# One transposing transfer becomes three TensorE transposes and a copy, with the later steps of the plan in another order

## The chip, the cores and the metric

The kernel runs on one core of a Trainium2 chip. The metric is the time of one execution on the device in microseconds (us), taken over several runs; the median counts. One further execution was recorded by the hardware profiler, and its rows are what the views of the profile show.

## What is computed

Clustered attention followed by a two-layer SiLU network. Four batches of 8 heads, 768 positions, head size 64; a query sees a key only if both have the same nearest of 16 centroids.

```python
q_assign = np.argmax(np.einsum('bhsd,hcd->bhsc', q_n, c_n), axis=-1)
k_assign = np.argmax(np.einsum('bhsd,hcd->bhsc', k_n, c_n), axis=-1)
mask = q_assign[:, :, :, None] == k_assign[:, :, None, :]
scores = np.where(mask, scale * np.matmul(q, k.transpose(0, 1, 3, 2)), -1000000000.0)
attn = softmax(scores)
x = np.matmul(attn, v).transpose(0, 2, 1, 3).reshape(B * S, H * D)     # 3072 x 512
h = x @ w_in                                                          # 512 -> 2048
out = (h * (1.0 / (1.0 + np.exp(-h)))) @ w_out                        # 2048 -> 512
```

The inputs and the output are float32; inside, operands are float16 and sums float32 in PSUM.

## The kernel before, in words

The whole order of the work is written out by hand. `plan` (L815) is a list of some 1,600 words, and the loop at L894 turns each word into the instructions of one step, in that order. An engine takes its own instructions in the order of the list; between engines only the data and the buffers decide. So TensorE, VectorE (DVE), ScalarE (ACT), GpSimd (POOL) and the queue of SyncE (SP), which issues nearly all transfers, are five lists that run beside one another and wait where they must.

A word is a step's name, a number, and behind a dot the engine (A, D or P) or the PSUM bank. For the steps z and o the letter isn't read (L799 to L803); for hi, v, ce, pe and u it chooses the engine.

For head n (n = 0 to 31, eight to a batch):

- `r` (L92) loads q and k, two transfers; `hi` (L103, L105 or L107 by engine) and `lo` (L112, VectorE) split them into two float16 parts.
- `ht` (L121) turns them by a transposing transfer on SyncE's queue into the tile `ab`.
- `l` (L159) multiplies them by the centroids on TensorE, `ls` (L168), `mx` (L188) and `ge` (L197) on VectorE find the nearest one.
- The result goes back into `ab` as additional rows. For heads 8 to 15 by `cm` and `ce` (L226, L237, L239, L240); for heads 16 on by `cs` (GpSimd, L204), `cx` (a transposing transfer on SyncE, L213, into `cdt`) and `cv` (a transfer that GpSimd issues, L217).
- `vl` (L271) loads v, and `v` (L277, L279) casts it.

Attention goes by units of one head, one half of the queries and two blocks of keys: `qk` (L336, two matmuls of 384 columns into `pS`, two buffers) and `ex` (the exponential on ScalarE, L341). `pv` n (L353, 36 matmuls) multiplies the exponentials of a pair of heads by v; n counts batch, half of the queries and pair of heads, so that 12 to 15 are the four pairs of batch 1's second half. `nm` (L363, L365) normalises the result on VectorE into `xn`.

The normalised rows must be turned before the network can use them, into one of the four row blocks of the tile `xt`. There are two ways, and the plan names one for each pair:

```python
def xn_t(i, c, bk=None):
...
    for t in range(NM):
        nc.tensor.transpose(px[:, ts(t, 128)], xn[:, 2 * t : 2 * t + 2, :].rearrange("p h d -> p (h d)"), ident)
def xn_d(i, c):
...
    nc.sync.dma_start_transpose(
        xts[b, c][:, i % H // 2, :].rearrange("p (t n) -> p t n", t=NM), xn.rearrange("p n d -> p (n d)")
    )
```

The first is the step `pt`, three transposes on TensorE into PSUM, followed by the step `pe` (`xn_ev`, L376), the copy into `xt` by ScalarE (L383) or VectorE (L385). The second is the step `xd`, one transposing transfer on SyncE's queue (L392). The first layer of the network, for batches 0 and 1, is `e` (L401, four matmuls of 384 columns, one for each row block of `xt`, in order: the fourth reads the last pair's rows), `t` (tanh on ScalarE, L413) and `g` (the gate on VectorE, L416). Steps e48 to e63 belong to batch 1's second half. Batches 2 and 3 form the same products with seven block products for eight: sums `T` and `ws`, products `y` (L467), mixing copies and sums `u` (L479, L481, L483) and `s` (SiLU on ScalarE, L489). The second layer is `m` (L559, eight matmuls), with the sums `S` (L572) on VectorE, and `z` and `o` (L581, L587, L590), which scale the result and send it out.

Buffers that bind steps together: `xn` 3, `hl` 4, `P` 13 (exponentials), `ab` 12, `cdt` 4, `tn` 3, and eight PSUM banks, two pairs of which hold `pS`.

Of the kernel before, what the change touches and what calls it, by code (L numbers as in the profile page):

```python
# [29 lines left out]
def kernel(  # L30
# [655 lines left out]
    def step(op, n, eng, banks):  # L686
# [167 lines left out]
        t58 e59.2 g58 t62 g62 t53 g53 hi25.A qk108 ex108 lo27 cx23 vl19 S22 t59 qk104 hi26.P ex104 cx22 e51.1 t51 g51
        m21.0 qk105 z20.A m22.3 ex105 v19.P qk110 ex110 vl22 vl27 m26 qk111 ex111 xd16 o20 l24.1 vl21 qk128 ex128
        e55.3 qk109 ex109 g59 e52.2 t52 cv22 lo26 ls24 S24 g52 qk113 ex113 z21.D lo25 pv17.1 nm17 r28 ht27 hi28.D
        v21.P r30 e54.2 t54 ht26 qk130 ex130 qk112 ex112 t55 cv23 m25 mx24 g54 qk116 e63.1 g55 ex116 qk124 r31 pv18.2
        ex124 nm18 z22.A qk127 ge24 ex127 qk126 ex126 v22.P e57.3 t57 m27.2 o23 g57 xd17 t63 hi30.D vl23 qk118 ex118
        g63 ht25 qk114 ex114 m23 o21.D v23.D lo28 v27.P qk117 ex117 l26.3 ls26 r29 cs24 cx24 qk115 e50.1 ex115 qk119
        ex119 e49.0 t49 ws5 qk138 pv19.3 lo30 ex138 t50 g49 vl29 g50 qk123 ex123 qk121 ex121 e48.0 l25.1 t48 ls25 mx25  # L860
        g48 qk122 ex122 m24 qk120 ge25 cv24 nm19 cs25 vl26 ex120 l27.1 ls27 qk125 m31.0 mx27 S33 qk129 ge27 ex125
        hi29.D pv20.3 mx26 ex129 vl24 qk132 ex132 qk136 ex136 m37 qk142 z30.D ex142 ge26 ht30 cx25 e61.1 nm20 cv25
        qk133 ex133 m32.3 lo29 ws6 ht28 t61 ws8 o30 qk139 ex139 g61 S31 qk134 S32 ex134 pv21.3 qk137 xd18 S43 nm21
        l30.1 cs27 cx27 qk135 cs26 S41 ls30 m36 ex137 xd19 ex135 cx26 xd21 qk140 ex140 ht29 z31.A pv22.3 qk141 ex141
        o22 v26.D qk143 S34 ws0 nm22 m35 ex143 hi31.P qk146 ex146 pv23.1 z32.D o33 qk148 ws1 ex148 qk149 xd20 ws12 ws2
        xd22 ws13 m41.2 z40.A ex149 m33 nm23 ws14 xd23 cv27 vl25 m34 qk154 ex154 m47 mx30 ge30 o31.A S42 qk145 ex145
        qk147 l28.3 o32 ex147 lo31 ws9 y161.1 ht31 l29.0 qk155 ex155 m46 z41.A cv26 qk150 qk144 ls28 ex150 ls29 mx29
        T20 T21 ex144 m45 mx28 y167.3 z42.A o43 y177.4 ws7 u170.A y197.4 m42.0 u190.D y171 u160.A u161.A y191 u171.A
        m44 ws15 T22 T23 ge29 y172 y162 y166 ws10 u191.A s160 S44 ws3 y176 s170 u162 u172 ge28 m43 o41.D o42 y165 u163
        y192 y196 s190 v29.D u192 o40 y164 y174 y163 y175 s162 s161 l31.2 u173 y187.3 s163 u180.D y195 s172 y181.0  # L870
        ls31 u181.A vl31 s173 y194 u193 y207.1 y173 y201.2 s171 y182 y186 cs30 s192 y237.4 u200.D u201.D cx30 y202
        s180 y193 s193 y206 u182 ws11 s200 s191 cs28 y184 s182 y185 y217.4 u202 y204 u183 u230.A y205 y231 u203 s183
        y183 s202 u210.A y221.3 u231.D y227.1 s203 v24.D cs29 cx29 y211 v31.A u220.D y203 y232 u211.A u221.D y236 s230
        y216 u232 y212 s210 u212 y222 y226 s220 u222 y235 y234 s181 v25.A s201 cx28 cv28 y214 u233 s233 y215 u213 y225
        u223 s232 s213 y224 s223 s212 mx31 m51.0 z50.A y223 ge31 s222 y233 s231 pv24.2 y213 s221 s211 m61.1 S53 S51
        S52 qk156 ex156 cs31 m52.3 qk153 ex153 m56 z51.A qk151 S54 ex151 qk152 nm24 m57 S63 ex152 qk172 ex172 m55
        z52.D cv30 qk162 ex162 cv29 qk161 ex161 vl28 v28.D m67 qk158 S61 o53 m54 vl30 z60.D ex158 qk171 ex171 qk181
        pv25.2 ex181 qk157 ex157 qk160 ex160 m53 qk159 S62 ex159 S73 nm25 qk174 m66 ex174 cx31 cv31 qk165 ex165 qk164
        ex164 pv26.2 qk163 ex163 S71 o50 o51.D nm26 xd26 xd25 qk167 ex167 m62.3 o52 qk166 ex166 m71.2 qk169 ex169
        qk168 v30.P pv27.0 ex168 z61.D qk173 qk170 ex173 m65 ex170 o60 qk189 nm27 S64 xd27 ex189 qk179 pv28.3 S72  # L880
        ex179 qk177 qk175 nm28 z62.D ex177 m63 S74 o63 qk178 ex175 ex178 z70.A qk176 ex176 m72.0 xd24 o70 qk182 ex182
        m76 qk184 ex184 qk183 ex183 pv29.3 nm29 xd29 qk180 ex180 qk185 ex185 m64 o62 z71.D qk190 ex190 qk188 ex188
        pv30.0 nm30 qk186 ex186 qk187 ex187 m77 qk191 ex191 m75 pv31.3 nm31 z72.D m73 xd28 pt31.0 o73 y241.3 m74
# [44 lines left out]
```

## Time and profile before

| | |
|---|---|
| runs before | 297.19 us median of 3 (296.39 to 299.04) |
| profiled execution | 297.06 us, with a span of 295.2 us from its first to its last instruction |
| granted TensorE clock | 1.00 |
| TensorE (PE) busy | 285.8 us (97%), 3353 matmuls |
| ScalarE (ACT) busy | 245.1 us (83%) |
| VectorE (DVE) busy | 224.5 us (76%) |
| GpSimd (POOL) busy | 70.1 us (24%) |
| transposing transfers on SyncE's queue | 24 ht, 22 xd, 16 cx |

A row of the timeline has the start in us from the beginning of the span, the length, the engine, the line of the kernel, the operation, what it writes and reads, and how many instructions were merged. In brackets stands how long the engine was idle before it and for whom it waited. A row of groups has the busy time and the mean length of one in ns, then the idle time ahead of the group. Matmuls overlap: one of 384 columns is shown with 0.326 us, and the next starts 0.163 us after it. "SPq" is SyncE's queue, with the time that issuing a transfer took there; how long it took to land is told apart from that.

### The profile page before, as it was taken

The page shows a single profiled execution, that of the slowest core. Times are in us where ns is not written, and L with a number is a line of the kernel's source. Part 1 is how long each engine was busy: PE and PEld are TensorE (multiplying, and loading weights), DVE is VectorE, ACT ScalarE, POOL GpSimd, SP SyncE. Part 2 cuts the span into 40 slices and gives each one's busy share as a digit, 9 for nine tenths or more (in the row PEclk, how much of TensorE's full clock was granted, in tenths as well). Part 3 has the DMA queues.
Part 4 walks back from the last instruction along what each step waited for, and adds up shares of the span by engine and source line. Part 5 has one row for each costly group of instructions (what it writes and reads, how often), then busy time and mean ns, then how long its engine had stood idle before and what let it go on. Part 6 is the DMA issues. An engine that isn't in the chain of part 4 may idle for free.

```text
span 295.2 us, 8436 instructions
## 1 busy us (share of the span) xinstructions
PE 285.8 (97%) x3353; PEld 208.2 (71%) x3353; DVE 224.5 (76%) x489; ACT 245.1 (83%) x431; POOL 70.1 (24%) x118
## 2 busy tenths in 40 slices
...
GB/s 207 290 273 232 178 195 189 216 248 196 189 265 153 182 177 196 187 195 188 178 231 194 189 141 96 197 48 143 40 30 2 64 64 76 73 36 3 36 56 124
DMA packets 76166, 44.11 MB, mean 149 GB/s; under 512 B 54288, under 2 KB 72496, under 8 KB 76128
## 3 DMA queue, kind: packets, MB, share of 16 engines
...
HBM read 27.30 MB, written 6.29 MB: 114 GB/s over the span
## 4 chain that ended last, share of the span: by engine, by line
PE 79%; DMA 7%; ACT 5%; DVE 4%; issue 2%; SPq 1%; POOLq 0%; DVEq 0%; ACTq 0%
PE pS L336 19%; PE xb L559 18%; PE ph L401 11%; PE pO L353 10%; PE gd L467 5%; PE psN L159 3%; PE yb L559 3%; DMA ab<-cd 3%; PE gx L467 3%; PE po L498 2%; PE gy L467 2%; ACT P L341 2%; DMA raw<-in_q_dram 1%; PE wb L559 1%; DVE hl L112 1%
## 5 line engine op out<-in xcount | busy, mean ns | idle before, releaser
L341 ACT ACTIVATE P<-pS 128x768 f16<-128x768 f32 x192 | 150.0, 816 | 17.4 <-PE pS L336 15.5
L336 PE MATMUL pS<-ab 128*128 128x384 f16 x384 | 87.1, 326 | 1.3 <-DMA ab<-cd 0.6
L401 PE MATMUL ph<-xt,win_s 128*128 128x384 f16 x256 | 49.8, 326 | 1.5 <-DMA xt<-xn 1.3
L336 PEld LDWEIGHTS <-ab 128*128 128x128 f16 x384 | 33.4, 98 | 16.5 <-issue 3.0
L353 PEld LDWEIGHTS <-P 128*128 128x128 f16 x1152 | 39.8, 97 | 4.4 <-DVE cd L239 0.4
L353 PE MATMUL pO<-vt,P 128*128 128x65 f16 x1152 | 41.2, 193 | 0.0
L416 DVE SCALAR_TENSOR_TENSOR gt<-tn,ph 128x384 f16<-128x384 f32 x64 | 34.0, 549 | 9.5 <-ACT tn L413 9.0
L559 PEld LDWEIGHTS <-gt 128*128 128x128 f16 x352 | 34.3, 98 | 7.4
L401 PEld LDWEIGHTS <-win_s 128*128 128x128 f16 x256 | 24.7, 98 | 17.0 <-issue 1.2
L112 DVE SCALAR_TENSOR_TENSOR hl<-raw,hl 128x768 f16<-128x768 f32 (+3 forms) x35 | 32.1, 917 | 0.6 <-ACT hl L103 0.4
L413 ACT ACTIVATE tn<-ph 128x384 f32<-128x384 f32 x64 | 30.2, 503 | 2.3 <-PE ph L401 2.1
L105 POOL TENSOR_SCALAR hl<-raw 128x768 f16<-128x768 f32 (+1 forms) x12 | 24.5, 2044 | 29.8 <-DVE mxn L188 14.6
L559 PEld LDWEIGHTS <-s 128*128 128x128 f16 x264 | 25.6, 98 | 5.3 <-DVE s L572 0.3
L559 PE MATMUL xb<-wout_s,gt 128*128 128x256 f16 x176 | 22.6, 273 | 0.0
L159 PEld LDWEIGHTS <-ab 128*128 128x128 f16 x496 | 18.0, 97 | 4.8 <-DMA ab<-hl 0.5
L559 PE MATMUL xb<-wc,s 128*128 128x256 f16 x160 | 20.7, 273 | 0.0
L363 DVE RECIPROCAL zr<-pO 128x6 f32<-128x6 f32 x32 | 6.1, 192 | 19.1 <-PE pO L353 18.9
L581 ACT ACTIVATE ot<-xb 128x256 f32<-128x256 f32 x33 | 12.6, 386 | 8.8 <-PE xb L559 8.6
L204 POOL TENSOR_SCALAR od<-od 128x96 f16<-128x96 f16 x16 | 9.8, 610 | 40.6 <-DVE od L197 40.4
L159 PE MATMUL psN<-stk,ab 128*128 128x32 f16 (+1 forms) x496 | 19.1, 186 | 0.1
L572 DVE TENSOR_TENSOR s<-gt 128x1024 f16<-128x1024 f16 x22 | 15.7, 716 | 4.5 <-PE xb L559 2.7
L365 DVE TENSOR_TENSOR xn<-pO,zr 128x384 f16<-128x384 f32 x32 | 17.8, 558 | 1.4 <-DMA xt<-xn 0.3
(128 smaller groups left out, 413.6 us busy)
## 6 DMA issues: line engine op xcount, KB each, us to landing
...
```

Source lines behind the costliest of these rows:

```text
L105: nc.gpsimd.tensor_scalar(out=o, in0=i, scalar1=QS, scalar2=None, op0=ALU.mult)
L112: nc.vector.scalar_tensor_tensor(out=hl[:, s, 1, :], in0=raws[job.name][:, s, :], scalar=QS, in1=hl[:, s, 0, :], op0=ALU.mult, op1=ALU.sub ...
L159: nc.tensor.matmul(L[:, n % 2, :, n // 2], ab[:, i, :], stk[:, job.groups[i // 3][0], x : x + w], start=(x == 0), stop=(x + w == 2 * HC),)
L336: nc.tensor.matmul(pS[:, e, 0:HALF], abs_[kj.name][:, kn, :], rhs, start=True, stop=True)
L341: nc.scalar.activation(out=P, in_=pst.pop(u)[:, :, 0:HALF], func=AF.Exp, bias=0.0, scale=ESC)
L353: nc.tensor.matmul(o[:, (2 * t + h) * VW : (2 * t + h + 1) * VW], Ps[i + h, c, j // 2][:, j % 2, ts(t, 128)], vtb[(i + h) % 13][:, j, 0:VW ...
L365: nc.vector.tensor_tensor(out=xn, in0=ov[:, :, 0:D], in1=zr.unsqueeze(2).to_broadcast([128, 2 * NM, D]), op=ALU.mult)
L401: nc.tensor.matmul(ph[:, 0:HALF], win_s[:, r, ts(fb, 128)], xts[b, c][:, r, :], start=(r == 0), stop=(r == NR - 1))
L413: nc.scalar.activation(out=tn, in_=phs[b, c, fb][:, 0:HALF], func=AF.Tanh, bias=0.0, scale=0.5)
L416: nc.vector.scalar_tensor_tensor(out=gt[:, fb, NM * c : NM * c + NM, :].rearrange("p t n -> p (t n)"), in0=tns.pop((b, c, fb)), scalar=1.0 ...
L467: nc.tensor.matmul(o[:, 0:HALF], w[:, r, :], x[:, r, :], start=(s in (7, 1) and r == 0), stop=(r == 1), skip_group_check=True)
L559: nc.tensor.matmul(o, self.lhs(l, f), self.rhs(r, f), start=(f == 0 and opens), stop=(f == HB - 1), skip_group_check=True)
```

## The change

The word `xd15` is gone. In its place stand `pt15.0` and `pe15.D`: the normalised values of pair 15 (batch 1, second half, last pair of heads) are turned by three TensorE transposes into PSUM bank 0 and copied by VectorE into `xt`. Everything up to the 329th word is as before; from there to the end the same steps stand in another order, and some run on another engine or in another PSUM bank. Among the letters that are read: nine of the mixing copies `u` go from ScalarE to VectorE and two the other way; of the casts `v`, six go from GpSimd to ScalarE, three from VectorE to ScalarE, three from VectorE to GpSimd, two from ScalarE to GpSimd, one from ScalarE to VectorE and one from GpSimd to VectorE; of `hi`, three go from GpSimd to ScalarE, one from GpSimd to VectorE, two from ScalarE to VectorE, and hi21 and hi23 go to GpSimd; four `ce` go from ScalarE to VectorE, and `pe6` from VectorE to ScalarE. No instruction is new but pt15 and pe15. The diff replaces lines of the plan alone; here are its first lines, and the stretch around the changed step of the old and of the new plan:

```diff
@@ -827,69 +827,69 @@
-        ex39 ex40 e7.1 e12.2 t12 ht11 g15 qk41 ex41 t7 g2 r15 wc6 e9.0 wc0 qk45 t9 ex45 hi13.P g12 wc12 pv6.3 g7 qk43
-        ex43 l8.2 ls8 qk47 b4.1 b5 mx8 ge8 g9 qk44 lo13 ex47 qk46 nm6 ex46 b0.2 l10.0 wc8 ex44 wc3 cm8.3 ce8.A b6
...
-        t19 t26 lo16 g18 r20 g19 vl15 ex54 ht16 qk56 ex56 l14.0 ls14 mx14 t21 g21 e16.2 t16 g16 ge14 g26 qk55 ex55
-        wc13 qk51 ex51 e28.0 l15.1 qk53 e17.2 ex53 t17 qk62 ex62 cm14.3 ls15 mx15 g17 ce14.A qk61 S3 ex61 v9.P ge15
-        wc7 pv8.1 nm8 qk63 ex63 m1.2 cm15.3 ce15.A hi17.D lo17 qk65 ex65 qk64 e30.1 t28 g28 m7 vl14 r19 xd8 v13.P wc14
-        ex64 wc2 wc15 t30 qk60 ex60 z0.D S13 g30 S11 S1 qk58 ex58 m2.3 qk77 o0 wc11 ex77 pv10.0 nm10 hi18.P qk57 ex57
-        vl18 m11.1 wc10 qk68 ex68 m17 S2 qk71 ex71 l16.3 ht17 qk75 ex75 r21 lo18 m6 qk66 ex66 qk70 ht18 pv9.0 S4 S12
-        qk67 z1.A ex70 xd10 ex67 z10.A m5 hi19.D ls16 lo19 qk73 z2.D o3 ex73 l17.3 ls17 m16 r22 z11.A qk83 ex83 ht19
-        nm9 hi20.D v14.P xd9 r23 mx17 m3 qk69 ex69 v15.P qk76 ge17 ex76 cs17 l18.3 m15 od2 lo20 ht20 mx16 qk78 cx17
-        z12.D o13 ls18 mx18 hi21.D ex78 pv11.0 nm11 qk88 qk74 ex88 ex74 m14 qk80 ex80 vl20 m4 ge16 cs16 qk82 cx16 ex82
-        qk72 ex72 S14 pt11.3 o12 o2 v20.P m13 lo21 pe11.A ht21 o11.A vl16 qk84 e42.0 ex84 hi22.D l19.3 t42 ge18 cs18
-        qk79 ex79 ls19 cx18 mx19 pv12.1 nm12 o1.A xd12 r24 ge19 lo22 qk81 ex81 e41.3 g42 qk86 ex86 e36.2 t36 g36 qk89
-        cs19 cx19 l20.1 ls20 ex89 ht22 qk87 ex87 mx20 ge20 e32.0 t32 g32 hi23.A qk91 ex91 pv13.2 nm13 v18.D e39.1 t41
-        vl17 g41 qk93 t39 g39 lo23 ht23 e35.0 t35 ex93 g35 e37.2 cv17 e43.3 t37 cv16 g37 cs20 cx20 t43 qk85 ex85 e46.1
-        g43 qk92 ex92 e44.0 t44 g44 r27 l21.2 ls21 r25 t46 qk90 ex90 e38.3 qk101 t38 pv14.0 qk95 ex101 mx21 ge21 v16.A
-        g38 ex95 nm14 xd13 xd14 qk94 ws4 ex94 l22.2 ls22 mx22 e34.3 g46 t34 g34 v17.D cv19 qk107 ex107 pv15.0 qk97
-        ex97 nm15 hi24.P lo24 e40.2 qk96 cv18 xd15 e33.1 l23.3 ex96 t40 qk106 ex106 ht24 ls23 cv20 ge22 qk131 ex131
-        cs22 r26 m12.0 t33 qk100 o10 ex100 mx23 e45.3 cs21 qk99 ex99 g33 ge23 t45 cs23 e47.0 e56.1 g40 t47 S23 g47
...
+        ex39 ex40 e7.1 e12.2 t12 ht11 g15 qk41 ex41 t7 g2 r15 wc6 e9.0 qk44 g7 t9 g9 pv6.3 nm6 wc0 wc8 ex44 qk42 ex42
+        b0.1 pt5.0 v11.P l8.3 ls8 mx8 hi13.P ge8 lo13 qk43 qk45 pe5.A b4.0 ex43 qk47 wc12 wc1 cm8.3 b1 ex45 g12 ce8.A
...
+        qk70 ex70 nm10 nm9 qk69 ex69 m16 qk71 l17.1 xd8 ex71 o3 qk68 ex68 hi19.D xd10 hi20.D r21 lo19 m3 z11.D xd9
+        ht19 qk72 wc10 ex72 qk78 v15.P pv11.3 lo20 ex78 ls17 r24 qk74 ex74 nm11 m15 ht20 z12.D qk81 ex81 mx16 pt11.1
+        qk76 ge16 ex76 cs16 o13 mx17 ge17 cs17 cx17 pe11.A m4 o2 l18.3 ls18 mx18 ge18 cs18 qk83 cx16 cx18 ex83 S14 r23
+        qk84 vl16 o1.D pv12.1 nm12 xd12 qk86 hi22.D ex84 e38.3 qk82 ex86 t38 g38 e46.2 ex82 qk80 t46 ex80 lo22 e39.1
+        qk90 g46 hi21.P e32.3 t39 ex90 g39 qk88 vl20 ex88 lo21 t32 ht22 e37.2 qk87 t37 g37 ex87 l19.1 cv17 ls19 mx19
+        g32 qk79 ge19 m14 ex79 e33.2 qk89 t33 qk85 e40.1 g33 ex89 t40 g40 l20.3 ls20 ex85 qk94 r26 pv13.2 hi24.A nm13
+        ex94 qk95 mx20 ex95 e35.1 t35 cs19 cx19 cv16 lo24 cv18 e44.3 t44 g35 ht21 qk93 hi23.P e43.2 t43 o12 qk92 ex92
+        g44 ex93 pv14.1 xd13 ge20 g43 m13 o11.D vl19 lo23 qk99 e34.3 ex99 nm14 e45.2 t45 g45 t34 g34 e36.0 t36 g36
+        cs20 cx20 qk91 ex91 e47.1 qk102 l22.2 ls22 mx22 ex102 t47 g47 ht23 e41.3 qk100 t41 g41 xd14 qk103 pv15.0 nm15
+        cv19 ex100 e42.2 ex103 t42 qk98 ex98 vl18 r27 hi26.P qk96 lo26 ht24 l21.1 ls21 ex96 m12.3 S23 mx21 qk104
+        pt15.0 ex104 qk106 ex106 pe15.D e59.1 r25 t59 ge21 qk97 cv20 g42 ex97 cs21 v16.P cx21 ht26 o10 g59 e58.0 t58
+        e62.2 v20.P g58 l23.3 ls23 t62 mx23 ge23 v17.A cv21 ge22 qk107 vl22 cs22 cx22 ex107 qk101 e60.1 t60 g62 g60
...
```

More of the change, by code (lines that the diff above doesn't have):

```diff
@@ L829 @@
         qk36 ex36 e10.1 e15.0 qk37 pt4.2 qk38 e2.3 t10 ex37 ex38 lo11 pe4.D ht9 r14 pv5.2 g10 t15 nm5 qk39 qk40 t2
-        ex39 ex40 e7.1 e12.2 t12 ht11 g15 qk41 ex41 t7 g2 r15 wc6 e9.0 wc0 qk45 t9 ex45 hi13.P g12 wc12 pv6.3 g7 qk43
-        ex43 l8.2 ls8 qk47 b4.1 b5 mx8 ge8 g9 qk44 lo13 ex47 qk46 nm6 ex46 b0.2 l10.0 wc8 ex44 wc3 cm8.3 ce8.A b6
-        v10.P qk42 pt6.3 b7 ht13 ls10 l9.0 mx10 ge10 pe6.D b1 hi12.A lo12 ex42 ls9 pt5.3 mx9 bo1 ht12 pe5.A pv7.0 ge9
-        nm7 v8.A hi14.A lo14 l11.3 cm10.1 b2 ce10.A pt7.0 pe7.A ls11 r16 cm9.1 ce9.A hi15.A mx11 ge11 b3 bo0 ht14 wc9
@@ L834 @@
-        e31.0 t31 g31 lo15 e20.3 cm11.1 ce11.A qk48 e25.2 l13.1 qk50 ls13 ex48 t20 g20 t25 g25 ex50 mx13 qk49 e29.0
-        t29 g29 vl9 ht15 e27.1 vl13 t27 l12.3 ls12 ex49 ge13 e23.2 t23 e24.0 t24 g27 cm13.3 ce13.A qk52 ex52 e22.1 t22
-        od1 g23 e19.2 mx12 ge12 cm12.3 ce12.A g24 r18 wc1 qk59 g22 e18.0 ex59 e26.3 qk54 t18 hi16.P v11.P e21.1 r17
-        t19 t26 lo16 g18 r20 g19 vl15 ex54 ht16 qk56 ex56 l14.0 ls14 mx14 t21 g21 e16.2 t16 g16 ge14 g26 qk55 ex55
-        wc13 qk51 ex51 e28.0 l15.1 qk53 e17.2 ex53 t17 qk62 ex62 cm14.3 ls15 mx15 g17 ce14.A qk61 S3 ex61 v9.P ge15
@@ L849 @@
-        g43 qk92 ex92 e44.0 t44 g44 r27 l21.2 ls21 r25 t46 qk90 ex90 e38.3 qk101 t38 pv14.0 qk95 ex101 mx21 ge21 v16.A
-        g38 ex95 nm14 xd13 xd14 qk94 ws4 ex94 l22.2 ls22 mx22 e34.3 g46 t34 g34 v17.D cv19 qk107 ex107 pv15.0 qk97
-        ex97 nm15 hi24.P lo24 e40.2 qk96 cv18 xd15 e33.1 l23.3 ex96 t40 qk106 ex106 ht24 ls23 cv20 ge22 qk131 ex131
-        cs22 r26 m12.0 t33 qk100 o10 ex100 mx23 e45.3 cs21 qk99 ex99 g33 ge23 t45 cs23 e47.0 e56.1 g40 t47 S23 g47
-        qk98 ex98 g45 qk102 e60.2 t60 hi27.P cx21 cv21 S21 t56 g56 ex102 pv16.0 nm16 qk103 ex103 e53.3 g60 e58.1 e62.0
@@ L854 @@
[L854 to L883, printed above, removed]
@@ L884 @@
-        pe31.D xd30 T30 y257.4 T31 T32 y247.0 o61.A o72 y277.4 u270.D u250.A y251 y287.1 u251.D u240.A u241.A T33 y242
-        y271 u271.D s240 y256 y246 u242 o71.A y252 y272 s250 u252 y276 s270 y245 u243 s243 y244 y254 u280.A u272 y255
-        y281.2 u253 u281.D y243 s242 y275 y274 s252 s241 y282 s280 u273 s272 s253 y286 u282 y261.0 y267.3 y253 s251
-        y273 s271 y284 y285 y297.4 y317.4 s282 u260.D u261.D y262 s273 y266 y307.1 s260 u283 s283 y283 u310.D u290.A
-        s281 y311 u311.A u262 y265 u263 y291 u291.A y301.2 s263 y316 y312 u300.A u301.A s310 u312 y264 y292 y296 s290
@@ L889 @@
-        y302 s300 y263 y306 u292 y315 y314 u302 s262 u313 y295 S83 y294 u293 s312 y304 s302 y305 s292 s261 m81.3 m87
-        z80.A u303 y303 y313 s311 S81 S82 S84 s301 y293 m86 z81.A s291 S93 m82.1 s303 m85 o80 m91.0 m97 z82.A o83 m84
-        s293 s313 S91 m92.2 S92 o82 z90.D m96 m83 S103 z91.A o90 o81.D m95 z92.A S101 m107.1 m101.2 z100.D S94 m93
-        S102 m106 o91.A m102.3 o93 z101.D m105 o100 S104 z102.D o103 m94 o92 m103 o101.D m104 o102
+        ex39 ex40 e7.1 e12.2 t12 ht11 g15 qk41 ex41 t7 g2 r15 wc6 e9.0 qk44 g7 t9 g9 pv6.3 nm6 wc0 wc8 ex44 qk42 ex42
@@ new lines @@
+        b0.1 pt5.0 v11.P l8.3 ls8 mx8 hi13.P ge8 lo13 qk43 qk45 pe5.A b4.0 ex43 qk47 wc12 wc1 cm8.3 b1 ex45 g12 ce8.A
+        qk46 ex46 l10.3 b5 ls10 mx10 l9.2 ls9 ht13 mx9 b6 b7 od1 ex47 ge9 cm9.3 hi12.A lo12 ce9.A bo1 pv7.2 nm7 hi14.A
+        b2 pt6.3 pt7.0 pe7.A ht12 r16 ge10 lo14 l11.2 ls11 ht14 mx11 b3 cm10.0 bo0 ce10.D pe6.A e25.3 t25 qk50 ex50
+        ge11 g25 qk48 hi15.D e27.2 cm11.1 t27 g27 ce11.A e20.0 t20 lo15 ex48 qk49 g20 e17.3 t17 l12.1 hi16.P ex49 vl13
+        e23.2 qk52 ls12 mx12 l13.0 ls13 g17 ex52 t23 g23 vl9 e31.1 t31 od2 qk75 e28.0 ex75 v8.P t28 g31 e18.3 t18 mx13
@@ new lines @@
+        qk51 ex51 qk53 v10.A e24.2 t24 ge12 g18 g28 l14.1 ls14 mx14 e22.3 qk59 ge13 ex53 cm12.0 ex59 ht15 r18 e29.1
+        t29 qk54 ex54 ce12.D g24 cm13.0 ce13.D g29 t22 g22 qk55 ex55 lo16 ge14 e19.2 t19 g19 v9.A e16.0 e30.1 t16 g16
+        qk57 r17 t30 qk56 e21.3 t21 m1.2 ex56 g30 wc15 wc13 r19 g21 ht16 l15.0 ls15 ex57 S3 pv8.1 vl17 qk58 nm8 cm14.3
+        ex58 ce14.A qk62 ex62 vl15 e26.0 mx15 t26 qk61 m7 ge15 cm15.1 hi17.D qk63 ex61 ce15.D pv9.3 qk65 vl14 z0.D g26
+        lo17 ht17 wc9 ex63 m2.1 S13 hi18.A qk60 o0 S1 ex65 m11.0 ex60 r20 qk64 m17 wc3 lo18 ht18 qk77 ex64 l16.1 v14.A
@@ new lines @@
+        ex77 v13.P S2 S4 qk73 ex73 wc11 m6 z1.A qk67 ex67 r22 ls16 qk66 z10.D ex66 wc14 pv10.1 wc7 wc2 m5 z2.A S11 S12
+        qk70 ex70 nm10 nm9 qk69 ex69 m16 qk71 l17.1 xd8 ex71 o3 qk68 ex68 hi19.D xd10 hi20.D r21 lo19 m3 z11.D xd9
+        ht19 qk72 wc10 ex72 qk78 v15.P pv11.3 lo20 ex78 ls17 r24 qk74 ex74 nm11 m15 ht20 z12.D qk81 ex81 mx16 pt11.1
+        qk76 ge16 ex76 cs16 o13 mx17 ge17 cs17 cx17 pe11.A m4 o2 l18.3 ls18 mx18 ge18 cs18 qk83 cx16 cx18 ex83 S14 r23
+        qk84 vl16 o1.D pv12.1 nm12 xd12 qk86 hi22.D ex84 e38.3 qk82 ex86 t38 g38 e46.2 ex82 qk80 t46 ex80 lo22 e39.1
@@ new lines @@
+        cv19 ex100 e42.2 ex103 t42 qk98 ex98 vl18 r27 hi26.P qk96 lo26 ht24 l21.1 ls21 ex96 m12.3 S23 mx21 qk104
+        pt15.0 ex104 qk106 ex106 pe15.D e59.1 r25 t59 ge21 qk97 cv20 g42 ex97 cs21 v16.P cx21 ht26 o10 g59 e58.0 t58
+        e62.2 v20.P g58 l23.3 ls23 t62 mx23 ge23 v17.A cv21 ge22 qk107 vl22 cs22 cx22 ex107 qk101 e60.1 t60 g62 g60
+        ex101 vl23 e63.0 S21 qk124 ex124 e53.3 qk105 t53 g53 e51.2 t51 v18.A g51 pv16.1 nm16 e55.3 cs23 ex105 cv22
+        qk128 t63 ex128 g63 v19.A m22.2 qk130 ex130 vl21 S22 m21.1 z20.A v23.P o20 qk109 ex109 qk110 ex110 vl28 v22.A
@@ new lines @@
+        m26 qk108 ex108 l24.0 hi27.D lo27 ht27 cx23 pv17.2 z21.D ls24 qk113 mx24 qk112 t55 v21.P l26.0 g55 ex113 m25
+        nm17 ls26 mx26 r28 cv23 ex112 xd16 xd17 qk111 ex111 qk131 ex131 e57.3 t57 e52.2 v28.A z22.D S24 qk126 ex126
+        m27.0 qk127 g57 pv18.3 o23 r30 hi25.D lo25 nm18 qk115 ht25 ex127 qk116 m24 o22 ex115 ex116 qk114 ex114 xd18
+        e61.3 qk117 t61 ex117 ge26 ge24 vl24 hi28.D e49.0 t49 lo28 qk119 t52 g49 ex119 cs24 g52 m23 g61 cx24 ws4
+        hi30.D cv24 qk118 ex118 e56.0 qk138 ex138 r31 t56 g56 lo30 pv19.2 o21.D nm19 qk121 l27.3 ls27 ex121 mx27 qk120
```

32 lines of the change are left out of this document (added).

## The prediction

> **What bounds the kernel now.** I read the busy time of each engine by stretches first, from 56.1 us on, which is where the first step of another order (the 329th) begins.
>
> ```profile
> span 295.2 us, 8436 instructions
> ...
> 56.10:120.00 63.90, 63.79 (x797) 46.67 (x796) 57.82 (x124) 55.55 (x97) 16.95 (x24) 1.00 0.94 204
> 120.00:130.00 10.00, 9.58 (x123) 6.29 (x121) 8.69 (x17) 9.25 (x18) 3.18 (x3) 1.00 0.89 200
> 130.00:139.00 9.00, 7.73 (x78) 5.05 (x74) 7.80 (x18) 6.50 (x11) 4.71 (x8) 1.00 0.81 170
> 139.00:230.00 91.00, 90.88 (x1030) 67.82 (x1028) 70.23 (x148) 81.04 (x143) 19.67 (x35) 1.00 0.56 123
> 230.00:262.00 32.00, 31.78 (x380) 23.35 (x377) 16.68 (x37) 26.20 (x44) 0.00 (x0) 1.00 0.25 72
> 262.00:295.20 33.20, 29.76 (x237) 22.87 (x234) 18.42 (x35) 17.30 (x43) 0.00 (x0) 1.00 0.15 49
> ```
>
> After the length of a stretch stand the busy times of PE, PEld, DVE, ACT and POOL, then the granted clock (1.00 everywhere) and the DMA share. TensorE (PE) bounds: it idles 0.11, 0.12 and 0.22 us in three long stretches, and 3.44 us in the last, nearly all of it the final output after the last matmul. Only 120 to 139 us shows more: 0.42 and 1.27 us. So a new order can win what those 19 us hold, and little besides. Everywhere else it can only keep or lose. VectorE is busy 179.64 us and ScalarE 195.85 us of 239.1: both have room on average.
>
> Next I read those 19 us on TensorE, in order of time.
>
> ```profile
> 126.51 0.81 PE L336 MATMUL pS<-ab 128*128 128x384 f16 x4
> 127.45 0.52 PE L159 MATMUL psN<-stk,ab 128*128 128x32 f16 x12
> 128.12 0.81 PE L401 MATMUL ph<-xt,win_s 128*128 128x384 f16 x4
> 129.08 0.50 PE L336 MATMUL pS<-ab 128*128 128x384 f16 x2 [0.15 <-DMA ab<-cdt]
> ...
> 131.81 0.81 PE L401 MATMUL ph<-xt,win_s 128*128 128x384 f16 x4
> ...
> 135.63 0.98 PE L401 MATMUL ph<-xt,win_s 128*128 128x384 f16 x5
> 137.07 0.54 PE L401 MATMUL ph<-xt,win_s 128*128 128x384 f16 x2 [0.46 <-DMA xt<-xn]
> 138.41 0.32 PE L401 MATMUL ph<-xt,win_s 128*128 128x384 f16 x1 [0.81 <-DMA xt<-xn]
> ```
>
> The busy time of a matmul overlaps the next one, so a wait is larger when taken from start to start. What a piece costs the engine stands in the chain that ended last.
>
> ```profile
> 109.60 0.65 PE pS L336 x4
> 110.25 0.17 PE px L374 x3
> 110.41 0.87 PE xb L559 x8
> ...
> 111.61 0.65 PE ph L401 x4
> 112.26 0.35 PE psN L159 x12
> ...
> 112.94 1.09 PE pO L353 x36
> ...
> 135.12 3.25 DMA xt<-xn
> ```
>
> With 0.163 us for each matmul of 384 columns, the five from 135.63 (e47 and the first product of e56) end at 136.44 and the next starts at 137.07: 0.63 lost, to xd13, whose rows e56's second product reads. The two from there end at 137.40 and the last starts at 138.41: 1.0 lost, to xd15, which was issued at 135.12 and took 3.25 us. That last product wants the pair of heads that the change turns on TensorE. Together 1.6 us. Before them 127.45 is 0.29 late (126.51 + 0.65), 128.12 is 0.32 late (127.45 + 0.35) and 129.08 is 0.31 late (128.12 + 0.65): 0.9 us, the first and the last of it for transfers that SyncE's queue issued late (ht22, cx19). So I read that queue.
>
> ```profile
> 94.41 1.60 SPq L121 DMA_TRANSPOSE ab<-hl  x1
> ...
> 122.92 1.17 SPq L213 DMA_TRANSPOSE cdt<-od  x1
> ...
> 130.04 0.57 SPq L92 DMA_DIRECT2D raw<-in_q_dram  x1
> ...
> 132.54 3.79 SPq L392 DMA_TRANSPOSE xt<-xn  x3
> ```
>
> From ht17 at 94.41 to xd13 at 132.54 it goes from one issue to the next without a pause: 33 issues (7 ht, 5 cx, 3 xd, and 18 plain ones for r, vl and o) in 38.1 us. In the plan, xd15 stands just ahead of e33, which TensorE began at 131.81; it was issued 3.3 us behind that place. **SyncE's queue is the cause of both losses.**
>
> **The change, part by part.** Removed is xd15. With it go the wait of 1.0 us for it and 1.2 us of SyncE. I also credit the 0.63 for xd13 and the 0.9 ahead of it, because the new order stretches those paths (xd13 to e59, cx19 to qk106, ht22 to l22); what comes in their place is costed below. Gain: 1.6 + 0.9 = 2.5 us.
>
> Added on TensorE is pt15: three transposes, 0.17 us by the row px above, on the engine that bounds. Added on VectorE is pe15, and whether it is hidden depends on what is queued ahead of it.
>
> ```profile
> L374 PE MATMUL px<-ident,xn 128*128 128x128 f16 x30 | 3.3, 219 | 0.0
> ...
> L363 DVE RECIPROCAL zr<-pO 128x6 f32<-128x6 f32 x32 | 6.1, 192 | 19.1 <-PE pO L353 18.9
> L365 DVE TENSOR_TENSOR xn<-pO,zr 128x384 f16<-128x384 f32 x32 | 17.8, 558 | 1.4 <-DMA xt<-xn 0.3
> L112 DVE SCALAR_TENSOR_TENSOR hl<-raw,hl 128x768 f16<-128x768 f32 x26 | 25.5, 980 | 0.0
> L168 DVE TENSOR_REDUCE L<-psN 128x192 f32<-128x384 f32 x24 | 13.2, 552 | 3.6 <-PE psN L159 3.6
> L572 DVE TENSOR_TENSOR s<-gt 128x1024 f16<-128x1024 f16 x22 | 15.7, 716 | 4.5 <-PE xb L559 2.7
> L188 DVE TENSOR_REDUCE mxn<-L 128x12 f32<-128x192 f32 x24 | 12.0, 500 | 0.5
> L385 DVE COPY xt<-px 128x384 f16<-128x384 f16 x7 | 2.5, 352 | 0.5 <-PE px L374 0.5
> ```
>
> From the end of pv15, VectorE has nm15 (0.19 + 0.56), lo26 0.98, ls21 0.55, S23 0.72, mx21 0.50 and pe15 0.35: 3.85 us. Until e59's fourth product, the first that reads this row, TensorE has e42 0.65, four qk 1.3, l21 0.35, m12 0.87, pt15 0.17 and three products 0.49: 3.8 us. So pe15 is level with its use: 0 to 0.3 us late if VectorE is on time, up to the whole 1.6 us again if it is not. I take 0, since the third product of e59 waits longer for something else:
>
> **xd14 stays a transfer, and is now the last one.** I ask how far SyncE is behind when it comes to it. From xd8 to the issue ahead of xd14 the new plan has 29 issues: 5 ht, 5 cx, 5 xd and 14 plain ones, so the same 15 transposes but four plain ones fewer. At 0.65 us each (0.57 and a gap) that is 38.1 - 2.6; two ht that became xd save 0.48 us each by these medians:
>
> ```profile
> L121 SPq DMA_TRANSPOSE ab<-hl x24: 1287/1681/7246, 47.8 to 189.1; - x24
> ...
> L392 SPq DMA_TRANSPOSE xt<-xn x22: 1178/1204/2393, 92.5 to 249.1; - x22
> ...
> DMA to landing us min/median/max: 2.3/2.5/4.8
> ```
>
> That leaves 34.5 us of SyncE. TensorE's work between the same two steps is 25 qk, 15 e, 4 pv, 5 m, 4 l and one pt: 8.1 + 9.8 + 4.4 + 4.4 + 1.4 + 0.2 = 28.2 us. SyncE would come 6.4 us late. The same sum for the old order, from ht17 to xd15, is 40.7 us (94.41 to 135.12) against 34.2 of TensorE's work (31 qk, 13 e, 6 pv, 8 m, 6 l, one pt), 6.5 us, where 3.3 were measured, as SyncE began ahead and TensorE was held up itself. Taking off the same 3.2 leaves 3.2. From xd14's place to the product that reads it TensorE has 5.1 us; the transfer takes 3.25 (as xd15) from its issue. Late by 3.2 + 3.25 - 5.1 = **1.4 us**. Its ends: 0, if SyncE is level (2.5 to land, 5.1 to cover it); 4.6, if the whole 6.4 us stands. I take 1.4, since the nearest row, xd15 itself, behaved so. While TensorE waits at e59, ScalarE's t59 and VectorE's g59 wait behind it, as t56 and g56 did.
>
> The other steps move, and some change engine: seven more mixing copies run on VectorE and seven fewer on ScalarE.
>
> ```profile
> L479 DVE COPY gy<-gx 128x384 f32<-128x384 f32 x4 | 2.3, 567 | 0.3
> ...
> L481 ACT ACTIVATE sb<-gd 128x384 f32<-128x384 f32 x5 | 2.4, 489 | 3.3 <-PE gd L467 3.2
> ```
>
> That is 7 x 0.57 = 4.0 us more for VectorE and 3.4 less for ScalarE, spread over stretches in which both have over 5 us to spare. Casts go both ways; on GpSimd four of hi leave and two come (hi21, hi23), and cs and cv queue behind those, on an engine that is busy 44.5 of 239.1 us. Their cover is TensorE's own work, and without it a step costs its length. For all other steps together I take a loss of 0.4 us: they can win at most the 0.45 us of the long stretches, and a new wait could be as dear as the dearest here, 1.6. The output's tail after the last matmul keeps its kind and length.
>
> Sum, against the profiled execution (span 295.2, time 297.06, so 1.9 around it): 297.06 - 2.5 + 0.17 + 1.4 + 0.4 = **296.5 us**. The median of the runs, 297.19, lies 0.13 above that execution.
>
> By the Trainium skill, VectorE: DVE Perf Modes, section The three transpose paths, one 128x128 transpose takes TensorE 390 ns and the transposing DMA 1309 ns. By that, pt15 would cost three times 390 ns, and the sum would be 1.0 us later, 297.5: a rule against the change. The trace does not agree: its transposes take 219 ns alone, and three in a row cost 0.17 us.
>
> **The rivals.**
> - *Clean.* SyncE is level at xd14; nothing takes the place of the waits. For it: from xd12 to xd14 only 12 issues stand beside 20 us of TensorE's work. Against: the 34.5 us. 297.06 - 2.5 + 0.17 = 294.7 us, and 294.2 or less if the long stretches gain too.
> - *The queue in full (the other side).* One mechanism: SyncE is 6.4 us behind at xd14, and e59 waits 4.6 us in place of 1.4. It makes the kernel slower than before from a backlog of about 4.0 us at xd14 on. 296.5 + 3.2 = 299.7 us. For it: 33 issues without a pause in this trace, and 17 issues from xd8 to xd12 beside 8 us of TensorE's work. Against: the 3.3 measured for xd15.
> - *It doesn't do what it says.* xd15 goes, but pe15 comes late behind lo26, S23 and mx21, and e59 loses the 1.6 us that e56 lost. 296.5 - 1.4 + 1.6 = 296.7 us if it covers xd14's wait, 298.1 if it comes on top.
>
> **How the numbers follow.** About 1% is what a measurement of this kernel can tell from no change, that is 294.2 to 300.2 us. Chances: forecast 0.45; clean 0.22, half of it below 294.2; the queue in full 0.20, rather more than half of it over 300.2, as waits behind it (ht24, cx21) may add to it; late pe15 0.13, a little of it over 300.2. Faster 0.11, same 0.74, slower 0.15. The forecast's own range, with xd14 between 0.5 and 2.5 late, is 295.6 to 297.6. For 8 times in 10 it reaches to the clean case and to the queue in full: 294.4 to 299.7.
>
> **What would show it.** In the profile of the changed kernel: no wait for xd15; pt15's three transposes in 0.17 us; TensorE's wait at e59 ahead of its third product on xt<-xn, some 1.4 us; no such waits as the three of 0.3 us; SyncE some 3 us behind at xd14; over 99% busy in the other long stretches. Wrong it would be if e59 waits for VectorE's copy instead, if TensorE stands still in a stretch that is full now, or if the mixing copies hold up the last 33 us.

## The result, and the profile after

The changed kernel takes 294.74 us (median of 20 runs, 292.93 to 296.43) against 297.19 us (20 runs, 295.02 to 300.46). The ratio is 0.9926, with a 95% interval of 0.9905 to 0.9948: 0.7% faster, inside the 1% that the forecast called "same". The profiled execution has a span of 292.0 us and took 293.75.

The busy time by stretches, the view that was read first before; columns as there (length, PE, PEld, DVE, ACT, POOL, clock, DMA share, GB/s):

```profile
56.10:120.00 63.90, 63.90 (x795) 46.26 (x794) 59.85 (x124) 56.38 (x97) 13.45 (x20) 1.00 0.92 206
120.00:130.00 10.00, 10.00 (x106) 6.84 (x104) 8.12 (x18) 8.77 (x18) 5.93 (x5) 1.00 1.02 211
130.00:139.00 9.00, 8.58 (x107) 6.11 (x106) 7.47 (x16) 8.02 (x14) 2.14 (x5) 1.00 1.13 208
139.00:230.00 91.00, 90.85 (x1045) 68.63 (x1044) 72.86 (x156) 82.35 (x146) 18.97 (x35) 1.00 0.56 122
230.00:262.00 32.00, 31.67 (x363) 22.78 (x361) 17.78 (x40) 25.35 (x44) 0.00 (x0) 1.00 0.20 55
262.00:292.00 30.00, 26.66 (x219) 21.18 (x217) 17.54 (x33) 13.70 (x33) 0.00 (x0) 1.00 0.16 54
```

The idle time between 120 and 139 us has fallen from 0.42 + 1.27 to 0.00 + 0.42 us. What is left of it stands ahead of e59's third product, and is a wait for a transposing transfer. TensorE in order of time, with the three transposes of pt15 at 133.92:

```profile
133.92 0.33 PE L374 MATMUL px<-ident,xn 128*128 128x128 f16 x3
134.09 0.49 PE L336 MATMUL pS<-ab 128*128 128x384 f16 x2
134.42 0.49 PE L401 MATMUL ph<-xt,win_s 128*128 128x384 f16 x2
135.33 0.48 PE L401 MATMUL ph<-xt,win_s 128*128 128x384 f16 x2 [0.42 <-DMA xt<-xn]
```

The transposes cost 134.09 - 133.92 = 0.17 us of TensorE. The first two products of e59 end at 134.42 + 0.33 = 134.75, and the third starts at 135.33: 0.59 us lost from start to start. VectorE around pe15, from the same stretch:

```profile
131.50 0.56 DVE L365 TENSOR_TENSOR xn<-pO,zr 128x384 f16<-128x384 f32 x1
131.98 0.95 DVE L112 SCALAR_TENSOR_TENSOR hl<-raw,hl 128x768 f16<-128x768 f32 x1
...
134.00 0.49 DVE L188 TENSOR_REDUCE mxn<-L 128x12 f32<-128x192 f32 x1
134.41 0.35 DVE L385 COPY xt<-px 128x384 f16<-128x384 f16 x1
```

The copy pe15 ends at 134.76. Without the wait ahead of it, e59's fourth product would have started at 134.42 + 3 x 0.163 = 134.91. So the turned pair is on time, by 0.15 us. The late one is xd14, here in SyncE's queue, with the view of the tile xt that tells how long its transfers took to land:

```profile
125.24 1.20 SPq L392 DMA_TRANSPOSE xt<-xn  x1
...
127.24 1.17 SPq L213 DMA_TRANSPOSE cdt<-od  x1
128.52 1.46 SPq L121 DMA_TRANSPOSE ab<-hl  x1
130.07 2.17 SPq L392 DMA_TRANSPOSE xt<-xn  x1
132.29 0.57 SPq L271 DMA_DIRECT2D vn<-in_v_dram  x1
...
DMA to landing us min/median/max: 2.7/4.0/5.2
```

The transfer at 125.24 is xd13, and xd14 is the one at 130.07. It was issued at 130.07, held the queue for 2.17 us and landed 5.2 us after its start, at 135.3. That is the time at which TensorE went on.

From the start times of all matmuls I made one table. A gap is the time from one start to the next less the median spacing of such matmuls in the kernel before; "waits" are the gaps between 120 and 150 us for SyncE's transfers or for the turned pair, "other" is all the rest behind step 329. One profiled execution in each row; the kernels of the lower rows are told below.

| kernel | time of that execution | waits | other gaps |
|---|---|---|---|
| before | 297.06 | 2.51 | 5.02 |
| before, again | 297.14 | 1.73 | 5.70 |
| changed | 293.75 | 0.59 | 4.27 |
| changed, again | 296.33 | 1.54 | 4.64 |
| old order, turn alone (three executions) | 295.32, 296.38, 297.70 | 0.46, 1.82, 2.77 | 4.68, 4.82, 4.78 |
| old order, two loads later | 296.37 | 1.33 | 5.63 |
| new order, no turn | 294.53 | 0 | 4.35 |
| new order, xd14 early (two executions) | 294.10, 293.37 | 0, 0 | 4.56, 4.46 |
| new order, no turn, xd14 early | 296.26 | 2.23 | 4.50 |
| new order, loads ahead of xd14 | 296.93 | 2.98 | 4.69 |
| new order, both pairs turned | 295.54 | 0.98 | 4.58 |

Two things stand in it. The waits differ by over 2 us between executions of one and the same kernel. And the other gaps are 5.1 us in the mean of the six profiles of the old order (4.7 to 5.7) and 4.5 us in the mean of the eight of the new one (4.3 to 4.7).

### The profile page after: what moved, and what is told of

It is laid out like the page before. It is cut to its first block, busy times and chain, and to the rows that moved or that the text cites. A ratio compares the mean times of both kernels' runs of the same rounds, so it can differ in the third digit from the quotient of the medians.

```text
span 292.0 us, 8452 instructions
## 1 busy us (share of the span) xinstructions
PE 284.4 (97%) x3356; PEld 208.4 (71%) x3356; DVE 228.3 (78%) x498; ACT 244.5 (84%) x427; POOL 66.7 (23%) x114
## 4 chain that ended last, share of the span: by engine, by line
PE 87%; DVE 4%; DMA 3%; ACT 3%; issue 1%; SPq 0%; DVEq 0%; ACTq 0%
PE pS L336 20%; PE xb L559 18%; PE ph L401 14%; PE pO L353 11%; PE gd L467 5%; PE psN L159 4%; PE yb L559 3%; PE gx L467 3%; PE po L498 2%; PE gy L467 2%; DMA xt<-xn 2%; DMA raw<-in_q_dram 1%; PE wb L559 1%; ACT P L341 1%; DVE hl L112 1%
## 5 line engine op out<-in xcount | busy, mean ns | idle before, releaser
L559 PEld LDWEIGHTS <-gt 128*128 128x128 f16 x352 | 34.2, 98 | 7.2
L401 PEld LDWEIGHTS <-win_s 128*128 128x128 f16 x256 | 24.4, 98 | 16.0 <-issue 0.9
L105 POOL TENSOR_SCALAR hl<-raw 128x768 f16<-128x768 f32 (+1 forms) x10 | 20.2, 2016 | 28.2 <-DMA raw<-in_k_dram 15.1
L467 PEld LDWEIGHTS <-win_s 128*128 128x128 f16 x128 | 12.3, 98 | 8.5 <-issue 0.8
```

What stands on the lines that cost most here:

```text
L105: nc.gpsimd.tensor_scalar(out=o, in0=i, scalar1=QS, scalar2=None, op0=ALU.mult)
L401: nc.tensor.matmul(ph[:, 0:HALF], win_s[:, r, ts(fb, 128)], xts[b, c][:, r, :], start=(r == 0), stop=(r == NR - 1))
L467: nc.tensor.matmul(o[:, 0:HALF], w[:, r, :], x[:, r, :], start=(s in (7, 1) and r == 0), stop=(r == 1), skip_group_check=True)
L559: nc.tensor.matmul(o, self.lhs(l, f), self.rhs(r, f), start=(f == 0 and opens), stop=(f == HB - 1), skip_group_check=True)
```

## The experiments

All ratios are to the kernel before, on the same chip, with 95% intervals. The diffs show only the words of the plan around each edit, without its line breaks.

**The changed kernel again**, beside its first neighbours, without an edit.

> The changed kernel itself, as the measure for its neighbours on the same chip. Ratio to the kernel before 0.9926 as measured first; in the profile TensorE waits at e59 ahead of its third product for xd14, some 0.6 us, and the three waits of 0.3 us of the old order are absent.

Measured: 0.9928 (0.9897 to 0.9959). In this execution the wait at e59 is far longer than in the first:

```profile
135.22 0.33 PE L374 MATMUL px<-ident,xn 128*128 128x128 f16 x3
135.39 0.49 PE L336 MATMUL pS<-ab 128*128 128x384 f16 x2
135.72 0.49 PE L401 MATMUL ph<-xt,win_s 128*128 128x384 f16 x2
137.58 0.48 PE L401 MATMUL ph<-xt,win_s 128*128 128x384 f16 x2 [1.38 <-DMA xt<-xn]
```

From 136.05 to 137.58, 1.54 us. SyncE's queue tells why; its first row is xd13, then come cx20, ht23 and xd14:

```profile
128.22 1.19 SPq L392 DMA_TRANSPOSE xt<-xn  x1
...
130.21 2.25 SPq L213 DMA_TRANSPOSE cdt<-od  x1
132.57 1.46 SPq L121 DMA_TRANSPOSE ab<-hl  x1
134.13 1.62 SPq L392 DMA_TRANSPOSE xt<-xn  x1
```

xd14 was issued at 134.13, 3.2 us behind its place in TensorE's order, where it was 0.4 us behind in the first profile. TensorE came to e59 1.3 us later than in the first profile (135.72 and 134.42). xd13 was issued 3.0 us later, so 1.7 us of the queue's further delay stood before cx20, which added 1.1: it took 2.25 us of the queue where it took 1.17 in the first profile.

**The turn alone**, in the old order:

```diff
-qk96 cv18 xd15 e33.1 l23.3 ex96 t40 qk106 ex106 ht24 ls23 cv20
+qk96 cv18 e33.1 l23.3 ex96 t40 pt15.0 qk106 ex106 ht24 ls23 pe15.D cv20
```

> The old order, with xd15 alone replaced by pt15 and pe15. Theory (SyncE's queue was behind, and turn and order each take away their own part): the wait of 1.0 us for xd15 goes, 0.17 us of transposes come, the 0.63 us for xd13 and the 0.9 us ahead of it stay; about 0.8 us gained, ratio 0.997. Rival A (the turn does all): the ratio of the whole change, 0.9926. Rival B (the order does all, and the turn is hidden anyway): 1.000.

Measured: 1.0002 (0.9966 to 1.0037). No change is shown, and the 0.997 of my theory, which lies inside the interval, can't be told from it; rival A, that the turn does all, is out. Its profile showed only 0.46 us of waits, in an execution of 295.32 us where the median was 296.76. Two more executions of it were profiled.

> The turn alone in the old order, a second look, since its profile showed 0.5 us of waits where its median showed no gain. Theory (the queue is still behind in most executions): waits for xd13 or xd14 at e56, or for cx21 at qk111, 1 to 2 us in sum. Rival (the copies of this kernel's transposes cost elsewhere): no such waits, and TensorE idle in other places than in the kernel before.

> The turn alone in the old order, a third look, for the same question: waits on SyncE's transfers between 126 and 150 us of 1 to 2 us in sum by the theory, none by the rival.

Measured: 296.38 and 297.70 us. TensorE's waits in the last of them, with VectorE's copy pe15:

```profile
128.08 0.52 PE L159 MATMUL psN<-stk,ab 128*128 128x32 f16 x12 [0.33 <-DMA ab<-hl]
129.43 0.50 PE L336 MATMUL pS<-ab 128*128 128x384 f16 x2 [0.18 <-DMA ab<-cdt]
...
133.33 0.81 PE L336 MATMUL pS<-ab 128*128 128x384 f16 x4
133.84 0.35 DVE L385 COPY xt<-px 128x384 f16<-128x384 f16 x1
134.24 1.03 PE L559 MATMUL yb<-wout_s,gt 128*128 128x256 f16 x8
...
138.81 0.73 PE L401 MATMUL ph<-xt,win_s 128*128 128x384 f16 x3 [1.42 <-DMA xt<-xn]
```

From the first execution to the third the waits rise by 2.77 - 0.46 = 2.3 us and the time by 2.4 us. The wait at e56 is for xd13 and xd14: with xd15 gone, other transfers of the same queue are the late ones. In this execution and the one of 296.38 us they cost e56 1.7 and 1.5 us, nearly as much as in the kernel before (1.6 and 1.7); in the one of 295.32 us they cost 0.2. The rival holds for a small part: in all three profiles the second-layer step m12, which writes the PSUM bank that pe15 empties, starts 0.26 us late for that copy (here 134.24, where 133.33 + 0.65 = 133.98 was due). So the turn costs 0.17 + 0.26 = 0.43 us in the old order. The waits for SyncE's transfers, 1.4 us in the mean of the three profiles against 2.1 before, fell by 0.7, not by 1.0, which leaves 0.3 us. Of the half microsecond that is missing from the expected 0.8, about one half went to the other transfers and one half to m12.

**The order alone**: the new order, pair 15 by a transposing transfer right behind xd14.

```diff
-xd14 qk103 pv15.0 nm15 cv19
+xd14 qk103 pv15.0 nm15 xd15 cv19
...
-mx21 qk104 pt15.0 ex104 qk106 ex106 pe15.D e59.1
+mx21 qk104 ex104 qk106 ex106 e59.1
```

> The new order with pair 15 turned by a transposing transfer again, issued right behind xd14. Theory: the transfer is issued near 132.3 us and lands at 136 to 137.5, while e59's last product could run at 135.5; 1 to 2 us more wait than in the changed kernel less 0.17 us, ratio 0.995 to 0.998. Rival A (the turn does all): 1.000. Rival B (the order does all): 0.992, as the changed kernel or 0.17 us better.

Measured: 0.9953 (0.9923 to 0.9983), in the range of the theory; rival A is out again. But its profile does not show what the theory said: in that execution xd15 was issued at 133.35 and landed 2.3 us later, just in time, and e59 did not wait at all (row "no turn" of the table). Whether it has such waits in its slower executions is open. The turn is worth 0.3 us in the new order by the medians (294.84 and 294.57 us on the same chip) and 0.7 by the ratios (0.9953 and 0.9928), less than the intervals tell apart.

**Both pairs turned**:

```diff
-ex99 nm14 e45.2 t45 g45 t34 g34 e36.0
+ex99 nm14 e45.2 t45 g45 pt14.1 t34 g34 pe14.D e36.0
...
-qk100 t41 g41 xd14 qk103
+qk100 t41 g41 qk103
```

> The changed kernel with pair 14 turned by TensorE too (pt14, pe14 in place of xd14). Theory: the 0.6 us wait at e59 goes for another 0.17 us of transposes, about 0.4 us under the changed kernel, ratio 0.991. Rival (the wait is not SyncE's but moves to VectorE's copies, which come late): no gain over the changed kernel, e59 or e47 waits for pe14 or pe15.

Measured: 0.9953 (0.9925 to 0.9981), where the theory said 0.991. The rival holds. The wait at e59 is gone, but a new one of 0.98 us stands ahead of e47, which writes the PSUM bank that pe14 empties, and pe14 comes late on VectorE behind two gates:

```profile
127.34 0.33 PE L374 MATMUL px<-ident,xn 128*128 128x128 f16 x3
...
128.12 1.02 DVE L416 SCALAR_TENSOR_TENSOR gt<-tn,ph 128x384 f16<-128x384 f32 x2 [1.48 <-ACT tn L413]
...
129.06 0.35 DVE L385 COPY xt<-px 128x384 f16<-128x384 f16 x1
...
129.46 0.81 PE L401 MATMUL ph<-xt,win_s 128*128 128x384 f16 x4 [0.82 <-DVE xt L385]
```

**The kernel before, profiled again**.

> The kernel before once more, one look, to see how far the waits between 126 and 139 us differ from one execution to the next. Theory: SyncE's issue times differ by a microsecond or more, and the waits at l22, e34, qk107 and e56 differ with them, between some 0.5 and 3 us in sum, while all other gaps of TensorE stay as they were to 0.1 us. Rival (the waits belong to the order and are fixed): 2.5 us again.

Measured: 297.14 us. The waits at l22, e34 and qk107 (0.9 us) are absent; e56's are 0.77 and 0.96. The gaps behind 150 us are those of the first profile, one by one within 0.02 us. Ahead of 120 us they are not: their sum is 1.5 us where it was 0.9, so "all other gaps stay" holds only for the later part. So the gaps behind 150 us come with the order, and the waits differ with SyncE's transfers from one execution to the next.

**Two loads later in the old order**: r27 and r25 (four issues) go behind xd15.

```diff
-t44 g44 r27 l21.2 ls21 r25 t46
+t44 g44 l21.2 ls21 t46
...
-qk96 cv18 xd15 e33.1
+qk96 cv18 xd15 r27 r25 e33.1
```

> The old order with only the loads r27 and r25 moved behind xd15 in SyncE's queue; nothing is turned by TensorE. Theory (the queue's backlog): xd13, xd14 and xd15 are issued 2.5 us earlier, e56's wait of 1.6 us goes, ratio 0.995 to 0.996. Rival (the gain lies in the order of the compute steps): 1.000.

Measured: 0.9987 (0.9954 to 1.0019); the theory's 0.995 to 0.996 lies at its lower end, and no gain is shown. The profile has xd15 issued at 132.9 in place of 135.1 and no wait at e56. It was given back 10 us later, at the next product that needs a transfer of the same queue (cx21, then cv21, then qk111):

```profile
145.19 1.04 PE L559 MATMUL xb<-wc,s 128*128 128x256 f16 x8
147.40 0.50 PE L336 MATMUL pS<-ab 128*128 128x384 f16 x2 [1.17 <-DMA ab<-cdt]
```

**Two loads ahead of xd14 in the new order**: the opposite edit in the changed kernel.

```diff
-t41 g41 xd14 qk103
+t41 g41 r27 r25 xd14 qk103
...
-qk98 ex98 vl18 r27 hi26.P
+qk98 ex98 vl18 hi26.P
...
-pe15.D e59.1 r25 t59
+pe15.D e59.1 t59
```

> The changed kernel with the loads r27 and r25 moved ahead of xd14 in SyncE's queue, all else as in the new order. Theory: xd14 is issued 2.5 us later and e59's wait grows by as much, to 3 or 4 us; ratio 0.9927 + 0.0084 = 1.001. Rival (landing or the shared DMA engines, not the queue): unchanged, 0.9927.

Measured: 1.0041 (1.0006 to 1.0076), all of the change's gain lost and more. Nothing but the place of four issues in one queue differs from the changed kernel:

```profile
134.66 0.49 PE L401 MATMUL ph<-xt,win_s 128*128 128x384 f16 x2
137.97 0.48 PE L401 MATMUL ph<-xt,win_s 128*128 128x384 f16 x2 [2.82 <-DMA xt<-xn]
```

The wait is 137.97 - 134.99 = 2.98 us, 1.4 and 2.4 us more than in the two profiles of the changed kernel, and the time rises by 1.0041 - 0.9928 = 0.0113, that is 3.4 us; where the rest of it lies is not shown. The rival, that landing or the shared DMA engines make the wait, would have left it as it was: here xd14 landed 3.0 us after its issue, sooner than in either profile of the changed kernel (5.2 and 3.4).

**xd14 early in the new order**: issued right behind nm14, ahead of cx20 and ht23; measured twice.

```diff
-ex99 nm14 e45.2
+ex99 nm14 xd14 e45.2
...
-qk100 t41 g41 xd14 qk103
+qk100 t41 g41 qk103
```

> The changed kernel with xd14 issued right behind nm14, ahead of cx20 and ht23 in SyncE's queue. Theory: xd14 is issued some 3 us earlier, e59's wait goes (0.6 and 1.5 us in the two profiles of the changed kernel), and the mean gains about 1 us: ratio 0.989 to 0.990. Rival (landing times, not the queue, make the wait): no gain, 0.9927.

> e4 once more beside e7, since its interval overlapped that of the changed kernel. Theory: 0.990 again, some 0.8 us under the changed kernel's 0.9927, no wait at e59. Rival (e4 drew well): 0.9927.

Measured: 0.9901 (0.9866 to 0.9935) and 0.9921 (0.9894 to 0.9948). In both profiles e59 runs through; here the first, where xd14 was issued at 128.16 and all four products follow one another:

```profile
134.75 0.33 PE L374 MATMUL px<-ident,xn 128*128 128x128 f16 x3
134.92 0.49 PE L336 MATMUL pS<-ab 128*128 128x384 f16 x2
135.24 0.81 PE L401 MATMUL ph<-xt,win_s 128*128 128x384 f16 x4
135.89 0.49 PE L336 MATMUL pS<-ab 128*128 128x384 f16 x2
```

This is the fastest version that was run. That it beats the changed kernel (0.9926 and 0.9928) is likely by the missing wait, but not shown: the intervals overlap.

**xd14 early without the turn**: the same edit on top of the order alone.

> The new order with xd14 issued right behind nm14 and pair 15 turned by a transposing transfer again: no transpose by TensorE, the queue relieved by order alone. Theory (the queue's order is what counts, the turn is worth at most what it takes from the queue): within 0.3 us of e4, ratio 0.990 to 0.992, no wait at e59 or under 0.5 us. Rival (the turn carries a part of its own): 1 us above e4, 0.993 to 0.995, with a wait for xd15 at e59.

Measured: 0.9975 (0.9949 to 1.0001), beside 0.9921 on the same chip. The rival holds here: with xd14 early and pair 15 not turned, e59's last product waits 2.23 us for xd15.

```profile
134.57 0.65 PE L401 MATMUL ph<-xt,win_s 128*128 128x384 f16 x3
137.29 0.32 PE L401 MATMUL ph<-xt,win_s 128*128 128x384 f16 x1 [2.07 <-DMA xt<-xn]
```

So the turn does carry a part of its own, once xd14 is out of the way: 0.5% between these two. The chain of this execution shows that it is not the queue's backlog:

```profile
131.83 0.04 DVE xn L365
...
132.71 4.55 DMA xt<-xn
```

VectorE's last step of nm15 began at 131.83 and took 0.56 us, to 132.39; xd15 was issued 0.3 us behind that. The product that reads it could have started at 134.57 + 3 x 0.163 = 135.06, so a queue that is level leaves the transfer 2.4 to 2.7 us, and it took 4.55. In the version with no turn it was issued as close to its use, took 2.3 and cost nothing. So the turn takes away a path that is too short for a slow landing.

## Why the prediction was right or wrong, point by point

**The number.** 294.74 us is "same", as forecast, and lies in the range for 8 times in 10 (294.4 to 299.7), 0.3 us from its end. It is outside the forecast's own range (295.6 to 297.6): the sum said 296.5. So it was the allowance for the clean rival that held the result, not the sum.

**What bounds, and the cause.** Right in the main. TensorE bounds, and its waits in the middle are for SyncE's transfers. Four issues moved ahead of xd14 cost 3.4 us; xd14 moved ahead of two transposes removed the wait in both profiles. But the queue's backlog is one of two causes. How long a transfer takes to land is the other: with a landing of 2.3 us neither the 0.59 us of the first profile nor the 2.23 us of the version with no turn and xd14 early would have been lost.

**The gain of 2.5 us.** The term was taken from one execution, and it is not a constant. A second profile of the same kernel has 1.7 us of waits, and the 0.9 us ahead of e56 is not among them. The mean of the two is 2.1.

**pt15 and pe15.** Right: 0.17 us on TensorE, and a copy that ends 0.15 us before its use, where the sum had it level to 0.3 us late, with the queue on VectorE that the sum listed.

**xd14 becomes the late one, by 1.4 us.** The mechanism is shown: e59 waits ahead of its third product, for xt, in both profiles, with 0.59 and 1.54 us, 1.07 in the mean. Inside the term two sizes moved against each other. In the first profile SyncE was only 0.4 us behind, not 3.2, but the transfer took 5.2 us to land, not 3.25. In the second it was 3.2 us behind, as put, with a landing of 3.4. That the mean of the two waits came near the term is in part luck. From xd8 to xd14 the queue took 31.4 us (98.71 to 130.07) and 34.2 (99.97 to 134.13), where the sum had 34.5. The sum's form holds: lateness and landing less 5.1 us gives 0.5, 1.5 and, with the two loads ahead, 2.9 us, where 0.59, 1.54 and 2.98 were measured.

**All other steps, a loss of 0.4 us.** This is the step that failed, in sign. The prediction held that other steps "can win at most the 0.45 us of the long stretches". The bound was read from busy time, in which a matmul of 0.326 us covers a gap of up to 0.16 us to the next. From the kernel before:

```profile
255.76 0.49 PE L467 MATMUL gy<-tx,ws 128*128 128x384 f16 x2
256.32 0.48 PE L467 MATMUL gy<-xt,win_s 128*128 128x384 f16 x2
```

Two matmuls need 0.33 us, yet the next starts 0.56 us after the first of them, and the row shows no wait. From start to start the old order has 5.0 us of gaps outside the waits, and the new order has 0.6 us less in the mean of all profiles. Behind 150 us, 14 gaps over 0.07 us come back in every profile of the old order and sum to 2.4 us; 11 come back in every one of the new order and sum to 2.0. These come with the order. Further ones, up to 0.6 us in sum, come and go: in one of the six profiles of the old order and in six of the eight of the new. What each of the moved steps gave of that was not taken apart.

**The sum.** Behind step 329, TensorE needs 235.3 us from e9 to its last matmul in the mean of the two profiles of before (235.35, 235.25) and 233.5 in the mean of the two of the changed kernel (232.85, 234.17): 1.8 us less, where 0.5 was forecast. By terms: waits 2.12 - 1.07 = 1.05, other gaps 5.36 - 4.45 = 0.9, less 0.17. Against the forecast the old waits gave 0.4 less (2.1, not 2.5), xd14 cost 0.3 less, and the other steps came out 1.3 better; the last is nearly the whole miss by these four profiles. Of its 0.9, 0.6 us is what the mean of all profiles bears out. The medians differ by 2.45 us. The 0.65 us beyond the profiles' 1.8 is not resolved by two executions of each.

**The rivals.** The clean rival's 294.7 is the measured number, but its mechanism is not what happened: xd14's wait took the place of half of the old ones, and about half of the time that the profiles show came from gaps that the prediction had not seen. That the two agree is luck. Late pe15 did not occur, though it did for pe14 in the version with both turned. The queue in full did not occur here; in the version with two loads ahead of xd14 something like it did, with xd14 5.1 us behind its place, a wait of 2.98 us and a time 0.4% above before.

**Turn or order.** In the old order the turn alone gains nothing that can be measured, and the new order alone gains 0.5% (0.9953). Which part is left for the turn depends on what else is late: 0.3 us by the medians and 0.7 by the ratios, neither clear of the noise, where xd14 stands late in the queue; 1.5 us by the medians (295.91 against 294.45) and 1.6 by the ratios (0.9975 against 0.9921) where xd14 is early.
